# Windowed attention and routed experts on one core: the exponentials of a tile one step later in ScalarE's queue, and all products with the values ahead of the turned exponentials on TensorE

## The chip, the cores and the metric

The kernel runs on 1 core of one Trainium2 chip. The time is the device time of one execution in microseconds (us). Five engines have a queue each and work through it in order: TensorE (PE; its weight loads are listed as PEld), VectorE (DVE), ScalarE (ACT), GpSimd (POOL) and SyncE (SP, which here only issues DMAs).

## The reference

```python
# attention, q k v: (8, 8, 576, 64), window 64
scores = scale * q @ k^T ; kept where 0 <= row - col < 64
attn = softmax(scores) ; out = attn @ v
# routed experts on x = out as (4608, 512)
logits = xn @ en.T / tau ; expert_idx = argmax(logits)
out[mask] = gate_w[mask, None] * (max(x[mask] @ w1[e], 0) @ w2[e])
```

## The kernel before, in words

The 4608 tokens are 36 tiles of 128. The program is laid out by hand: `stages(s)` (L538) emits, for s = 0 to 34, one step of a software pipeline over the tiles, and every engine runs its instructions in the order of emission. After the loop an epilogue, also written out by hand, ends the last tiles between the first products of the experts. Then come the experts, group by group, each product as three of split operands (L916, L976).

A tile T goes through these stations, each with the step s in which it is emitted:

- s = T: `scores` (L213, PE, into the one PSUM tile `score`), `own_scores` (L220, ACT, copies the half of the scores that belongs to the tile's own keys), `all_scores` (L223, DVE, puts the other half in by a mask), `maxima` (L227, DVE), `less_max` (L231, POOL, subtracts the maximum in place), `exponentials` (L234, ACT, in place). The exponentials are the last but one thing that ScalarE gets in the step (in eight even steps, 14 to 28, a copy of a weight half for the experts, L629, follows; VectorE then subtracts it, L630).
- s = T + 1: `attn_transposes` (L243, PE, turns the exponentials into the PSUM tile `back`), `attn_copy` (L253, ACT), `attn_prev` (L256, DVE) and `attn_own` (L259, POOL, in place on what `attn_copy` wrote), which make the two masked operands.
- s = T + 2: `values_other` (L279, PE, needs `attn_prev`), `values_mine` (L293, PE, needs `attn_own`), then `x_out` (L317, L318, L321, DVE, divides by the sums).
- s = T + 3: `x_transposes` (L336, PE, into `xback`), `xT_evac` (L342, ACT), `squares` (L329, ACT). Later: logits, the choice of an expert (`choose`, L400 to L404, DVE), ranks (L421 to L425, PE; L456 to L471, DVE) and `place`, an indirect DMA of the row to its expert's place (L480, POOL). `choose` and the ranks come once in four steps for tiles 0 to 27.

In a step s TensorE's order is `scores(s)`, at times `logits_four`, `values_other(s-2)`, `attn_transposes(s-1)`, `x_transposes(s-3)`, small products of the routing, `values_mine(s-2)`. ScalarE's is `own_scores(s)`, `attn_copy(s-1)`, `xT_evac(s-3)`, `squares(s-3)`, the issue of a load of k, `exponentials(s)`, at times the weight copy. VectorE's is `all_scores(s)`, `maxima(s)`, `attn_prev(s-1)`, `x_out(s-2)`, the routing's work, at times L630. GpSimd's is `less_max(s)`, `attn_own(s-1)`, `place`, and once in four steps small routing work. SyncE issues the loads of q, v and the weights.

Of the kernel before, what the change touches and what calls it, by code (L numbers as in the profile page):

```python
# [27 lines left out]
NT = N // P  # L28
# [55 lines left out]
def attention_moe(ctx, tc, q, k, v, emb, tau, w1, w2, kc, kt, out):  # L84
# [83 lines left out]
    def load_q(T, engine=nc.sync):  # L168
        if T < NT:
            engine.dma_start(qT[:, T % RQ], q[T].rearrange("p (u c) -> p u c", u=4))  # L170
# [5 lines left out]
    def load_v(T):  # L176
        if T < NT:
            nc.sync.dma_start(vb[:, T % RV], v[T])

    def vblock(g):  # L180
        return vb[:, g // 2 % RV, g % 2]
# [4 lines left out]
    def scores(T):  # L186

        for z in range(2):
            if (2 * T + z) % NB == 0:
                for hp in range(2):  # L190
                    o = score[64 * z:64 * z + 64, hp].rearrange("p (u c) -> p u c", u=4)[:, :, :WIN]
                    nc.tensor.matmul(o, lhsT=ones[64 * hp:64 * hp + 64, :64],
                                     rhs=low[64 * hp:64 * hp + 64].rearrange("p (u c) -> p u c", u=4),
                                     start=True, stop=True)
        at = T % RK * KT
        for u in range(4):
            for hp, z in sides:
                pr, o = slice(64 * hp, 64 * hp + 64), score[64 * z:64 * z + 64, hp, u * P:(u + 1) * P]
                qz = qT[pr, T % RQ, u, z * WIN:(z + 1) * WIN]
                own = kT[pr, at + u * P + z * WIN:at + u * P + (z + 1) * WIN]  # L200
                if (2 * T + z) % NB == 0:
                    parts = [(o[:, WIN:], own)]
                elif z:
                    parts = [(o, kT[pr, at + u * P:at + (u + 1) * P])]
                else:
                    was = (T - 1) % RK * KT + u * P + WIN
                    if at:
                        hop = KT - WIN
                        parts = [(o, kT[pr, was:was + 2 * hop].rearrange("p (a c) -> p a c", a=2)[:, :, :WIN])]
                    else:  # L210
                        parts = [(o[:, :WIN], kT[pr, was:was + WIN]), (o[:, WIN:], own)]
                for to, keys in parts:
                    nc.tensor.matmul(to, lhsT=qz, rhs=keys, start=True, stop=True)  # L213
# [4 lines left out]
    def own_scores(T):  # L218
        sm[T] = ap.tile([P, 4, 2, WIN], F32, name="sm", bufs=3)
        nc.scalar.copy(sm[T], sv[:, :, :, 1])  # L220
# [12 lines left out]
    def exponentials(T):  # L233
        nc.scalar.activation(sm[T], sm[T], AF.Exp, scale=0.125)  # L234
# [3 lines left out]
    def attn_transposes(T):  # L238

        pT[T] = back.rearrange("p (u c) -> p u c", u=4)  # L240
        t = sm.pop(T).rearrange("p u h c -> p u (h c)")
        for u in range(4):
            nc.tensor.transpose(pT[T][:, u], t[:, u], ident)  # L243
# [7 lines left out]
    def attn_copy(T):  # L251
        aM[T] = ap.tile([P, 2, 4, P], F32, name="aM", bufs=2)
        nc.scalar.copy(aM[T][:, 0], pT[T])  # L253
# [15 lines left out]
    def values_other(T):  # L269

        px[T] = banks_of(T)
        other = aM[T][:, 1]
        g = 2 * T
        for u in range(4):
            for hp, z in sides:
                if z == 0 and g % NB == 0:
                    continue
                pr, pz = slice(64 * hp, 64 * hp + 64), slice(64 * z, 64 * z + 64)
                nc.tensor.matmul(px[T][hp][pz, u * (D + 1):(u + 1) * (D + 1)], lhsT=other[pr, u, pz],  # L279
                                 rhs=vblock(g - 1 + 2 * z)[pr, u], start=u == 0, stop=(g + z) % NB == 0 and u == 3)  # L280

    def values_mine(T):

        mine = aM.pop(T)[:, 0]
        g = 2 * T
        first = [(g + z) % NB == 0 for z in range(2)]
        halves_ = slice(0, 64), slice(64, P)
        for u in range(4):
            rows = halves_[:1] if first[1] else halves_ if first[0] or u > 1 else [slice(0, P)]
            for hp in range(2):  # L290
                pr = slice(64 * hp, 64 * hp + 64)
                for pz in rows:
                    nc.tensor.matmul(px[T][hp][pz, u * (D + 1):(u + 1) * (D + 1)], lhsT=mine[pr, u, pz],  # L293
                                     rhs=vblock(g)[pr, u], start=u == 0 and first[0] and pz.start == 0, stop=u == 3)
# [59 lines left out]
    def logits_four(G):  # L354

        a, b = GROUPS[G]
        for c in range(4):
            for T in range(a, b):
                j = 32 * (T - a)
                nc.tensor.matmul(plT[j:j + 32], lhsT=embT[:, c], rhs=xT[T][:, c], start=(c == 0), stop=(c == 3))  # L360

    def four_copy(G):
        turned_back[G] = ap.tile([P, P], F32, name="lT", bufs=1)
        nc.scalar.copy(turned_back[G], plT)

    def four_back(G):
        nc.tensor.transpose(plq.rearrange("p g e -> p (g e)"), turned_back.pop(G), ident)
# [165 lines left out]
    def warm(n, to=back):  # L533

        for _ in range(n):
            nc.tensor.matmul(to[:, :P], lhsT=ones, rhs=ones, start=True, stop=True)

    def stages(s):  # L538

        def there(d):  # L540
            return 0 <= s - d < NT

        def ending(d):
            return [G for G, (a, b) in enumerate(GROUPS) if b + d == s]

        def turned():
            if there(1):
                attn_transposes(s - 1)
                attn_copy(s - 1)

        scores(s)
        if s < 3:
            warm(12, side[1])
        own_scores(s)
        if s == 33:
            x_hi(0)
        four = [G for G in ending(3) if len(range(*GROUPS[G])) == 4]
        for G in four:
            logits_four(G)
            four_copy(G)  # L560
        load_q(s + RQ)
        if there(2):
            values_other(s - 2)
        load_v(s + RV - 3)
        for f in wsteps.get(s, ()):
            f()
        if s > 3:
            turned()
        if there(3):
            x_transposes(s - 3)  # L570
        for G in four:
            four_back(G)
        if s - 4 in (28, 29):
            logits(s - 4, side[(s + 1) % 2][:, :E])
        due = [G for G, (a, b) in enumerate(GROUPS) if s == (b + 5 if b - a == 4 else b + 4)]
        for G in due:
            if len(range(*GROUPS[G])) == 4:
                ranks(G)
        if there(2):
            values_mine(s - 2)  # L580
        all_scores(s)
        maxima(s)
        if s < 3:
            warm(12, side[1])
        if there(3):
            xT_evac(s - 3)
        for G in four:
            four_out(G)
        if s - 4 in (28, 29):
            nc.scalar.copy(x_rows(s - 4, s - 3)[:, 0, C_LOG:C_LOG + E], side[(s + 1) % 2][:, :E])  # L590
        less_max(s)
        if there(3):
            squares(s - 3)
        load_k(s + RK - 1, nc.scalar)
        if s > 3:
            attn_prev(s - 1)
            attn_own(s - 1)
        for G in due:
            if len(range(*GROUPS[G])) == 4:
                rank_base(G)  # L600
        if there(2):
            x_out(s - 2)
        if s in (32, 33):
            x_turned(s - 32)
        if 0 < s <= 3:
            turned()
            attn_prev(s - 1)
            attn_own(s - 1)
        for G in due:
            if len(range(*GROUPS[G])) == 2:  # L610
                ranks(G)
            ranks_out(G)
        for G, (a, b) in enumerate(GROUPS):
            for T in range(a, b):
                if s == (T + 9 if b - a == 4 else b + 4):
                    place(T)
        if s == 33:
            x_lo(0)
        for G in ending(3):
            choose(G)  # L620
            tokens(G)
            count(G)
        exponentials(s)
        if s == 33:
            x_hi(1)
            x_lo(1)
        if s in wsplit:
            c, at = wsplit[s]
            nc.scalar.copy(w1h[c][:, at], w1raw[c][:, at])  # L629
            nc.vector.tensor_tensor(out=w1l[c][:, at], in0=w1raw[c][:, at], in1=w1h[c][:, at].bitcast(F32), op=ALU.subtract)  # L630
        if 1 <= s < 7:
            blanks(s - 1)
# [175 lines left out]
    def x_hi(a):  # L808
        xh, xl, t = x_half(a)
        nc.scalar.copy(xh, t)  # L810
# [509 lines left out]
```

## Time and profile before

| | us |
|---|---|
| median of 3 runs (lowest, highest) | 628.2 (624.93, 630.13) |
| the profiled execution | 622.73 |
| its span in the profile | 621.0 |
| PE busy in the span | 593.6 (96%) |
| DVE, ACT, POOL busy | 429.5, 354.7, 232.4 |

The profile is of one execution. A busy time counts when an engine has an instruction under way. The loop over the tiles takes about the first 160 us, and the experts the rest. The granted TensorE clock is shown as a share of full speed.

### The profile page before, as it was taken

The page shows a single profiled execution, that of the slowest core. Times are in us where ns is not written, and L with a number is a line of the kernel's source. Part 1 is how long each engine was busy: PE and PEld are TensorE (multiplying, and loading weights), DVE is VectorE, ACT ScalarE, POOL GpSimd, SP SyncE. Part 2 cuts the span into 40 slices and gives each one's busy share as a digit, 9 for nine tenths or more (in the row PEclk, how much of TensorE's full clock was granted, in tenths as well). Part 3 has the DMA queues.
Part 4 walks back from the last instruction along what each step waited for, and adds up shares of the span by engine and source line. Part 5 has one row for each costly group of instructions (what it writes and reads, how often), then busy time and mean ns, then how long its engine had stood idle before and what let it go on. Part 6 is the DMA issues. An engine that isn't in the chain of part 4 may idle for free. (4 is left out here: it accounts for less than half of the span.)

```text
span 621.0 us, 17807 instructions
## 1 busy us (share of the span) xinstructions
PE 593.6 (96%) x6836; PEld 528.8 (85%) x6836; DVE 429.5 (69%) x883; ACT 354.7 (57%) x567; POOL 232.4 (37%) x224
## 2 busy tenths in 40 slices
PE   8899988889899999999999999999999999999995
PEld 7687777778799898989988999899889998998884
DVE  2778888888888658686566775756765677657623
ACT  3566766666542447466466664645676466636533
POOL 2567878787833133213203331142122331222011
PEclk9999999999999999999999999999999999999999
DMA  8887888885535588886786897839778877775351
GB/s 270 276 228 238 298 264 267 244 253 152 202 114 204 134 275 279 241 269 243 245 283 208 265 295 257 271 132 327 249 242 246 277 267 222 245 262 196 114 168 38
DMA packets 85789, 143.75 MB, mean 231 GB/s; under 512 B 15797, under 2 KB 36021, under 8 KB 85696
## 3 DMA queue, kind: packets, MB, share of 16 engines
q1 hardware_dynamic: 74560, 112.87, 58.0%
q0 software_dynamic: 6000, 19.18, 8.1%
q10 hardware_dynamic: 5136, 10.49, 5.6%
q8 instruction: 55, 0.90, 0.6%
q14 instruction: 38, 0.31, 0.2%
HBM read 123.23 MB, written 20.05 MB: 231 GB/s over the span
## 5 line engine op out<-in xcount | busy, mean ns | idle before, releaser
L916 PE MATMUL ph<-xh,w1h 128*128 128x256 f32 x576 | 162.0, 281 | 1.3 <-DVE rk L456 1.3
L916 PE MATMUL ph<-xh,w1l 128*128 128x256 f32 x576 | 161.9, 281 | 1.0 <-DVE w1l L159 1.0
L916 PE MATMUL ph<-xl,w1h 128*128 128x256 f32 x576 | 161.4, 280 | 0.3 <-POOL xl L814 0.3
L988 POOL DMA_INDIRECT out<-o,rest x39 | 49.3, 1265 | 219.9 <-ACT o L985 206.3
L976 PE MATMUL po<-w2h,hh 128*128 128x512 f32 x312 | 122.2, 392 | 0.0
L976 PE MATMUL po<-w2h,hl 128*128 128x512 f32 x312 | 121.8, 390 | 0.0
L976 PE MATMUL po<-w2l,hh 128*128 128x512 f32 x312 | 121.6, 390 | 0.0
L930 DVE SCALAR_TENSOR_TENSOR hl<-ph,hh 128x512 fp32r<-128x512 f32 x78 | 53.4, 689 | 92.9 <-ACT hh L926 92.7
L159 DVE TENSOR_TENSOR w2l<-w2raw,w2h 128x1024 fp32r<-128x1024 f32 x80 | 94.7, 1220 | 24.3 <-ACT w2h L156 24.0
L916 PEld LDWEIGHTS ph<-xh,w1h 128*128 128x128 f32 x576 | 108.1, 188 | 2.1 <-issue 1.4
L916 PEld LDWEIGHTS ph<-xh,w1l 128*128 128x128 f32 x576 | 108.3, 188 | 1.6 <-DVE w1l L159 1.4
L916 PEld LDWEIGHTS ph<-xl,w1h 128*128 128x128 f32 x576 | 108.3, 188 | 1.4 <-POOL xl L814 0.5
L156 ACT CAST w2h<-w2raw 128x1024 fp32r<-128x1024 f32 x80 | 81.5, 1049 | 39.7 <-PE po L976 32.0
L159 DVE TENSOR_TENSOR w1l<-w1raw,w1h 128x1024 fp32r<-128x1024 f32 x76 | 89.2, 1236 | 11.0 <-ACT w1h L156 10.3
L814 POOL TENSOR_TENSOR xl<-xt,xh 128x512 fp32r<-128x512 f32 x37 | 47.8, 1293 | 100.4 <-ACT xh L810 100.4
L926 ACT ACTIVATE hh<-ph 128x512 fp32r<-128x512 f32 x78 | 46.1, 595 | 57.1 <-PE ph L916 43.4
L156 ACT CAST w1h<-w1raw 128x1024 fp32r<-128x1024 f32 x76 | 73.9, 1047 | 0.0
L976 PEld LDWEIGHTS po<-w2h,hl 128*128 128x128 f32 x312 | 58.6, 188 | 12.6
L976 PEld LDWEIGHTS po<-w2l,hh 128*128 128x128 f32 x312 | 58.6, 188 | 11.5
L976 PEld LDWEIGHTS po<-w2h,hh 128*128 128x128 f32 x312 | 58.6, 188 | 11.5
L810 ACT CAST xh<-xt 128x512 fp32r<-128x512 f32 x39 | 24.1, 620 | 54.6 <-DVE xt L799 53.9
L231 POOL TENSOR_TENSOR sm<-sm,st 128x512 f32<-128x512 f32 x36 | 37.5, 1041 | 36.1 <-DVE st L227 31.6
(208 smaller groups left out, 836.1 us busy)
## 6 DMA issues: line engine op xcount, KB each, us to landing
w2raw<-in_w SPq DMA_DIRECT2D x76, 512.0 KB
w1raw<-in_w SPq DMA_DIRECT2D x72, 512.0 KB
xb<-xs SPq DMA_DIRECT2D x156, 64.0 KB
v<-in_v SPq DMA_DIRECT2D x36, 260.0 KB
qT<-in_q SPq DMA_DIRECT2D x36, 256.0 KB
kT<-in_k ACTq DMA_DIRECT2D x32, 256.0 KB
w1raw<-in_w SPq DMA_DIRECT2D x8, 256.0 KB
w2raw<-in_w SPq DMA_DIRECT2D x8, 256.0 KB
```

The source lines that it names most:

```text
L156: nc.scalar.copy(hi[c], raw[c])
L159: eng.tensor_tensor(out=lo[c], in0=raw[c], in1=hi[c].bitcast(F32), op=ALU.subtract)
L231: nc.gpsimd.tensor_tensor(out=t, in0=t, in1=st.pop(T).unsqueeze(2).to_broadcast([P, 8, WIN]), op=ALU.subtract)
L810: nc.scalar.copy(xh, t)
L814: eng.tensor_tensor(out=xl, in0=t, in1=xh.bitcast(F32), op=ALU.subtract)
L916: nc.tensor.matmul(o, lhsT=ww[c][:, f * P:(f + 1) * P], rhs=xx[:, c, :n], start=(c == 0 and i == 0), stop=(c == 3 and i == 2))
L926: nc.scalar.activation(hh, ph[g, part], AF.Relu)
L930: nc.vector.scalar_tensor_tensor(out=hl, in0=ph.pop((g, part)), scalar=0.0, in1=hh.bitcast(F32), op0=ALU.max, op1=ALU.subtract)
L976: nc.tensor.matmul(po[a], lhsT=xx[:, f, at], rhs=ww[f // 2][:, f % 2], start=(f == 0 and i == 0), stop=(f == 7 and i == 2))
L988: d = nc.gpsimd.indirect_dma_start(out=out, out_offset=bass.IndirectOffsetOnAxis(ap=tok, axis=0), in_=o, in_offset=None, bounds_check=N - ...
```

## The change

`exponentials(s)` is no longer emitted at the end of step s, but in step s + 1 right behind `own_scores(s + 1)`, for tiles 3 to 33 (tiles 0 to 2 and 34 stay where they were). `values_mine(s - 2)`, which stood behind the transposes and the routing's small products, is emitted right behind `values_other(s - 2)`, ahead of `attn_transposes(s - 1)`. So ScalarE's order in a step becomes `own_scores(s)`, `exponentials(s-1)`, `attn_copy(s-1)`, `xT_evac(s-3)`, `squares(s-3)`, and TensorE's becomes `scores(s)`, `values_other(s-2)`, `values_mine(s-2)`, `attn_transposes(s-1)`, `x_transposes(s-3)`. VectorE's, GpSimd's and SyncE's orders stay.

```diff
         own_scores(s)
+        if s > 3:
+            exponentials(s - 1)
         if s == 33:
             x_hi(0)
...
         for f in wsteps.get(s, ()):
             f()
+        if there(2):
+            values_mine(s - 2)
         if s > 3:
             turned()
...
             if len(range(*GROUPS[G])) == 4:
                 ranks(G)
-        if there(2):
-            values_mine(s - 2)
         all_scores(s)
         maxima(s)
...
             count(G)
-        exponentials(s)
+        if s < 3 or s == NT - 2:
+            exponentials(s)
```

## Rows read from the trace of the kernel before

**Rows 1.** Busy time of each engine in three stretches: in the loop over the tiles, and in two behind it. Columns: stretch and its length, busy time (instructions) of each engine, granted TensorE clock, share of the DMA engines, GB/s.

```profile
69.60:137.80 68.20, 60.01 (x1619) 50.55 (x1614) 57.91 (x136) 46.97 (x106) 53.93 (x54) 1.00 0.85 258
...
165.00:185.00 20.00, 19.89 (x353) 18.15 (x352) 15.74 (x52) 9.37 (x18) 9.88 (x16) 1.00 0.39 125
185.00:240.00 55.00, 53.96 (x377) 49.02 (x376) 40.38 (x131) 24.89 (x38) 16.05 (x15) 1.00 0.67 213
```

**Rows 2.** Who waited for whom in the loop (27.5 to 160 us): total us, times, longest.

```profile
ACT sm L234 <- POOL sm L231: 31.7, 29, 1.9
...
PE back L243 <- ACT sm L234: 7.2, 19, 0.5
```

**Rows 3.** The subtraction of the maximum on GpSimd in steps 4, 14, 29 and 33, from the timeline (start us, duration us); it marks the pace.

```profile
27.50 1.04 POOL L231 TENSOR_TENSOR sm<-sm,st 128x512 f32<-128x512 f32 x1 [1.36 <-DVE st L227]
...
69.58 1.04 POOL L231 TENSOR_TENSOR sm<-sm,st 128x512 f32<-128x512 f32 x1
...
137.76 1.04 POOL L231 TENSOR_TENSOR sm<-sm,st 128x512 f32<-128x512 f32 x1 [0.64 <-DVE st L227]
...
155.07 1.03 POOL L231 TENSOR_TENSOR sm<-sm,st 128x512 f32<-128x512 f32 x1 [0.95 <-DVE st L227]
```

**Rows 4.** The timeline of one step (scores of tile 24 at 110.09 us), all engines, instructions in order of start; a run of alike instructions is one row.

```profile
109.21 1.06 PE L293 MATMUL odd<-v,aM 64*128 64x65 f32 x24
...
110.09 1.05 PE L213 MATMUL score<-kT,qT 64*64 64x128 f32 x32
...
110.92 0.69 DVE L321 TENSOR_TENSOR xmore<-odd,sums 128x512 f32<-128x512 f32 x1
110.96 0.65 PE L279 MATMUL even<-v,aM 64*64 64x65 f32 x32
111.07 1.27 POOL L259 TENSOR_TENSOR aM<-aM,cs 128x512 f32<-128x512 f32 x1
111.13 0.63 ACT L234 ACTIVATE sm<-sm 128x512 f32<-128x512 f32 x1 [0.63 <-POOL sm L231]
...
111.53 0.18 DVE L400 TENSOR_REDUCE m<-xr 128x4 f32<-128x32 f32 x1
...
111.67 0.57 ACT L220 COPY sm<-score 128x512 f32<-128x512 f32 x1
111.74 0.65 DVE L401 TENSOR_TENSOR c<-xr,m 128x32 f32<-128x32 f32 x1
...
111.81 0.66 PE L243 MATMUL back<-cs,sm 128*128 128x128 f32 x4 [0.21 <-ACT sm L234]
...
112.51 0.59 ACT L253 COPY aM<-back 128x512 f32<-128x512 f32 x1 [0.27 <-PE back L243]
...
112.84 0.54 PEld L293 LDWEIGHTS even<-v,aM 64*64 64x64 f32 x16 [0.17 <-issue]
...
112.98 0.72 DVE L223 COPY_PREDICATED sm<-cs,score 128x512 f32<-128x512 uint32 x1
112.99 0.59 ACT L342 COPY xfour<-xback 128x512 f32<-128x512 f32 x1
...
113.47 0.64 ACT L329 ACTIVATE sq<-xmore 128x512 bf16<-128x512 f32 x1
...
113.81 0.69 DVE L227 TENSOR_REDUCE st<-sm 128x8 f32<-128x512 f32 x1
...
114.41 0.68 DVE L256 TENSOR_TENSOR aM<-back,cs 128x512 f32<-128x512 f32 x1
114.57 1.04 POOL L231 TENSOR_TENSOR sm<-sm,st 128x512 f32<-128x512 f32 x1 [0.66 <-DVE st L227]
115.01 0.16 DVE L317 TENSOR_SCALAR sums<-even 128x8 f32<-128x8 f32 x1
...
115.44 0.69 DVE L321 TENSOR_TENSOR xmore<-even,sums 128x512 f32<-128x512 f32 x1
115.57 1.27 POOL L259 TENSOR_TENSOR aM<-aM,cs 128x512 f32<-128x512 f32 x1
```

**Rows 5.** VectorE's part of the ranks, which comes once in four steps, and the mask that follows it, from the timeline.

```profile
101.45 0.18 DVE L456 TENSOR_TENSOR rk<-even,cs 128x32 f32<-128x32 f32 x1
...
102.59 0.76 DVE L465 TENSOR_TENSOR rk<-rk,oh 128x32 f32<-128x32 f32 x1
...
103.68 0.72 DVE L223 COPY_PREDICATED sm<-cs,score 128x512 f32<-128x512 uint32 x1
```

**Rows 6.** The weight copy and its subtraction in the loop, by line (27.5 to 160 us): form, count, busy us and mean ns, idle time before.

```profile
L630 DVE TENSOR_TENSOR w1l<-w1raw,w1h 128x512 fp32r<-128x512 f32 x8 | 5.5, 692 | 6.8 <-ACT w1h L629 6.2 <-DMA kT<-in_k 0.7
L629 ACT CAST w1h<-w1raw 128x512 fp32r<-128x512 f32 x8 | 4.8, 604 | 0.0
```

**Rows 7.** Step 3, in which `attn_copy` and `attn_prev` of tile 2 were late, from the timeline.

```profile
24.21 0.59 ACT L253 COPY aM<-back 128x512 f32<-128x512 f32 x1 [2.51 <-DMA qT<-in_q]
...
24.83 0.69 DVE L256 TENSOR_TENSOR aM<-back,cs 128x512 f32<-128x512 f32 x1 [1.52 <-ACT aM L253]
```

**Rows 8.** The product of L465 with GpSimd idle (the first row; GpSimd's `attn_own` had ended at 157.34) and with GpSimd's queue full (the second), and the GpSimd instruction that ended just before the second did, from the timeline.

```profile
157.43 0.15 DVE L465 TENSOR_TENSOR rk<-rk,oh 128x32 f32<-128x32 f32 x1
...
162.09 2.95 DVE L465 TENSOR_TENSOR rk<-rk,oh 128x16 f32<-128x16 f32 x1
...
163.72 1.27 POOL L259 TENSOR_TENSOR aM<-aM,cs 128x512 f32<-128x512 f32 x1
```

## The prediction

> **What bounds the kernel now.** I read the stretches first. Behind the loop TensorE has no room: it is busy 19.89 of 20.00 us and 53.96 of 55.00 us at the full clock [rows 1]. So what the loop loses or gains is passed on to the end one for one, and only the loop has to be worked out. In the loop no engine is full: of 68.20 us TensorE is busy 60.01, VectorE 57.91, GpSimd 53.93, ScalarE 46.97 [rows 1]. A stretch like that is paced by a loop of waits through several engines. The waits say where: ScalarE stood 31.7 us in 29 steps with the exponentials at the head of its queue, waiting for GpSimd's subtraction, and TensorE 7.2 us in 19 steps for the exponentials [rows 2].
>
> The loop is read from one step [rows 4], from start to start: exponentials to the next own-scores copy 111.67 - 111.13 = 0.54 (the copy stands behind them in the queue, and its scores had been ready since 110.09 + 1.05 = 111.14), copy to mask 0.57 + 0.05, mask to maxima 113.81 - 112.98 = 0.83, maxima to subtraction 114.57 - 113.81 = 0.76, subtraction to exponentials 1.04 + 0.04. Sum 3.83 us per step. VectorE's work for the routing and the weight copy come on top. The pace shows it: steps 4 to 14 and 29 to 33, without weight copies, take (69.58 - 27.50 + 155.07 - 137.76) / 14 = 4.24 us, or 16.97 for four steps; steps 14 to 29 take (137.76 - 69.58) / 15 = 4.545, or 18.18 for four [rows 3].
>
> **The change, part by part.**
>
> *Removed.* The own-scores copy no longer stands behind the exponentials, so the loop of 3.83 us is cut, and so is the weight copy's 0.60 us [rows 6], which stood in it between the two. The exponentials' own work (0.63) is the same. DMA issues keep their order: the load of k was and is issued behind the squares, the loads of q and v on SyncE's own queue.
>
> *Added.* `values_mine` now stands ahead of the transposes and needs `attn_own`. GpSimd runs `attn_own` of the tile before right behind the subtraction: 111.07 + 1.27 = 112.34, while `values_other` is through at 110.96 + 0.65 = 111.61 [rows 4]. So at the old pace TensorE waits 0.73 us there; before, it waited 0.21 us (0.38 in the mean, 7.2 / 19, [rows 2]) for the exponentials. Behind the waiting products stand the transposes, the x transposes and the next scores; the exponentials themselves are ready in time and cost nothing, hidden under this wait and the 0.88 us of `values_mine`.
>
> *The new loop.* It spans two steps: mask, maxima, subtraction, `attn_own`, `values_mine`, transposes, `attn_copy`, `attn_prev`, `x_out`, next mask but one. Start to start [rows 4]: 0.83 + 0.76 + 1.00 (114.57 to 115.57) + 1.27 + 0.05 (a handover) + 0.88 (`values_mine` to the next block, 109.21 to 110.09) + 0.70 (111.81 to 112.51) + 0.59 + 0.05 + 0.60 (114.41 to 115.01) + 0.43 (115.01 to 115.44) + 0.61 (110.92 to 111.53) = 7.77 us, or 15.54 for four steps.
>
> VectorE's routing work lies in it once in four steps each. Ranks: 0.18 and from L465 to the mask 103.68 - 102.59 = 1.09 [rows 5]; choice: 112.98 - 111.53 = 1.45 [rows 4]; together 2.72. Part of that is not work: L465 takes 0.15 when GpSimd is idle, 0.76 beside `attn_own` and 2.95 until GpSimd's queue has a gap [rows 5, 8], so 0.61 of its time and about 0.65 - 0.15 = 0.50 of L401's [rows 4] is blocking by GpSimd. Without it: 2.72 - 1.11 = 1.61. Four quiet steps then take 17.15 to 18.26. Both shares are likely to stay in part, since `attn_prev` comes later against `attn_own`; I take the middle, 17.7: 0.73 more than 16.97. There are 14 such steps, 3.5 fours: +2.6 us.
>
> The two waits in which `attn_prev` stands for `attn_copy` are the weak point of this sum: the timeline shows it plainly in step 3, where DVE idled 1.52 us and started at 24.83, right after the copy's end at 24.80 [rows 7]; elsewhere the copy was done long before. If it holds in every step, the loop is 7.77; if not, 0.59 + 0.05 fall out, 1.28 per four steps, and the quiet steps end at 16.4, a gain of 2.0 us. By the Trainium skill (PSUM — Partial Sum Buffer, "PSUM bank collisions raise a hardware error") two engines may not touch one bank and quadrant at once, two reads included, so a copy on ScalarE and a product on VectorE out of `back` have to be kept apart in every tile: by that rule the sum is the first. The row agrees in the one step where it can be seen, and I keep the first by the row.
>
> *Steps with weight copies.* Here the loop can go through ScalarE: `values_mine` 0.88, transposes to x copy 112.99 - 111.81 = 1.18, to the squares 113.47 - 112.99 = 0.48, squares 0.64 [rows 4], weight copy 0.60 + 0.05, subtraction on VectorE 0.69 [rows 6], then 0.83 + 0.76 + 1.00 + 1.27 + 0.05 as above: 8.43 for two steps, 16.9 for four. L630 now comes while `attn_own` runs, has two inputs in SBUF like L465, and would be blocked like it by some 0.6: 18.1. The loop through the ranks (17.15 to 18.26) runs beside it and the slower sets the pace, so the bounds are 17.15 and 18.26; I take 18.1, because the rows show blocking whenever such an add met `attn_own`. That is 0.1 less than 18.18 for 3.75 fours: -0.4 us.
>
> **Sum:** +2.6 - 0.4 = +2.2 us. On the profiled execution: 622.73 + 2.2 = 624.9 (its span 621.0 + 2.2 = 623.2); it lies 5.5 us under the median of the runs shown. On that median: 628.2 + 2.2 = 630.4 us.
>
> **The rivals.**
>
> 1. *TensorE's new wait counts in full* (slower). The 0.73 us take the place of 0.38, and every step is 0.35 longer: 29 steps x 0.35 = +10.2, 638.4 us. For it: TensorE is the busiest engine of the loop. Against it: the copy of the scores started 0.53 us after its scores were done [rows 4], so a later TensorE has that slack first. It decides from the point at which the scores end later than VectorE comes free for their mask.
>
> 2. *The lock the other way round* (slower). L630 starts first and GpSimd's adds stand for it, up to 0.69 in 8 steps [rows 6] on the subtraction's path: +5.5 on top of +2.2, 635.9 us. For it: VectorE's adds and GpSimd's do exclude each other [rows 5, 8]; against it: the rows show only VectorE as the one that waits. The Trainium skill (SBUF — State Buffer, "Who interferes with whom") has the port pair go to whoever issues first, whole, so by it this is possible; no run here shows it.
>
> 3. *The loop is cut and nothing takes its place* (faster). Then TensorE's own queue paces: start to start 0.87 + 0.85 (110.96 to 111.81 at most) + 1.03 (111.81 to 112.84) + 0.88 = 3.6, and about 0.3 per step for the small products, 3.9 for 29 steps against (155.07 - 27.50) / 29 = 4.40: -14.5, 613.7 us. Against it: `attn_own` ends 0.73 us behind `values_other` already.
>
> 4. *A smaller gain*: `attn_prev` doesn't wait for the copy and L630 isn't blocked: -2.0 and (16.9 - 18.18) x 3.75 = -4.8 (were the loop through the ranks also without the copy): -6.8, 621.4 us at the most; half of it is more likely, 625.
>
> **How the numbers follow.** About 1% (6.3 us) is what a measurement of this kernel can tell from no change. Chances: the forecast 0.58; rival 1 0.15; rival 2 0.07; rival 3 0.07; rival 4 0.13, of which 0.04 past 1%. So faster 0.07 + 0.04 = 0.11, slower 0.15 + 0.07 = 0.22, same 0.67. The likeliest gives 630.4. Its own bounds: low +0.18 x 3.5 - 1.03 x 3.75 = -3.2; high +1.29 x 3.5 + 0.08 x 3.75 = +4.8, and 0.17 us for the issue of `values_mine` [rows 4] in each loop of two steps, 14.5 x 0.17 = +2.5: 625.0 to 635.5. Widened towards rivals 1 and 4 and for the spread of the runs: 623.5 to 637.5.
>
> **What would show it.** ScalarE's wait at L234 for L231 should all but vanish (from 31.7 us), TensorE's for L234 too; a new wait of L293 for L259 of 0.3 to 1.0 us per step should stand in their place; L256 should wait for L253 in most steps; the quiet steps should take about 4.4 us, those with weight copies about 4.5, and everything behind 162 us should keep its length. It is wrong if the pace of the loop changes by more than 0.2 us per step either way, if L293 doesn't wait, or if the experts' part changes by more than 2 us.

## The result, and the profile after

The kernel after takes 631.8 us in the median of 20 runs, the kernel before 628.66 us beside it: ratio 1.0061 with a 95% interval of 1.0045 to 1.0078, that is 3.8 us longer (2.8 to 4.9). The ratio goes by the means, 632.2 and 628.4 us, without one of the 20 runs of after, which took 1465.84 us; so it says a little more than the medians, which lie 3.1 us apart. The forecast was 630.4 us, +2.2. A second series gave 632.35 us and 1.0058 (1.0040 to 1.0077).

The profiled executions don't show this number: their spans are 621.0 us before and 628.3 us after. Why they lie further apart is answered by a second profile of each kernel below. The loop is to be read first, and there the two waits of [rows 2] are gone and others stand in their place. First the waits of the kernel after in the same stretch, 27.5 to 160 us (total us, times, longest):

```profile
ACT aM L253 <- PE back L243: 39.1, 27, 2.3
DVE aM L256 <- ACT aM L253: 12.8, 16, 2.1
...
PE odd L293 <- POOL aM L259: 6.9, 9, 1.1
...
PE even L293 <- POOL aM L259: 5.0, 9, 1.0
```

and three groups of its instructions there, by line (form, count, busy us and mean ns, idle time before, ended by whom); lines from 555 on stand two or three further down than before, so L632 and L633 answer to L629 and L630:

```profile
L234 ACT ACTIVATE sm<-sm 128x512 f32<-128x512 f32 x29 | 18.7, 644 | 0.4 <-POOL sm L231 0.2
L633 DVE TENSOR_TENSOR w1l<-w1raw,w1h 128x512 fp32r<-128x512 f32 x8 | 9.6, 1203 | 0.0
...
L465 DVE TENSOR_TENSOR rk<-rk,oh 128x32 f32<-128x32 f32 x6 | 2.2, 363 | 0.0
```

ScalarE's wait for the subtraction fell from 31.7 us to 0.2. Its idle time now lies ahead of the next copy (39.1 us at L253, for the transposes, where before it was 5.4): the same engine waits as long as before (31.7 + 5.4 us), one instruction later. TensorE, which had waited 7.2 us for the exponentials, waits 6.9 + 5.0 = 11.9 us in 18 steps for `attn_own`. VectorE waits 12.8 us in 16 steps for `attn_copy`; in the kernel before that was 0.2 us in all.

The pace, by the subtraction in steps 4, 14, 29 and 33 as in [rows 3] (start us, duration us):

```profile
26.70 1.04 POOL L231 TENSOR_TENSOR sm<-sm,st 128x512 f32<-128x512 f32 x1 [1.33 <-DVE st L227]
...
71.58 1.05 POOL L231 TENSOR_TENSOR sm<-sm,st 128x512 f32<-128x512 f32 x1
...
140.00 1.03 POOL L231 TENSOR_TENSOR sm<-sm,st 128x512 f32<-128x512 f32 x1 [0.70 <-DVE st L227]
...
157.54 1.03 POOL L231 TENSOR_TENSOR sm<-sm,st 128x512 f32<-128x512 f32 x1 [0.42 <-PE back L243]
```

Steps 4 to 33 take 157.54 - 26.70 = 130.84 us, before 127.57: +3.3. The 14 quiet steps take (44.88 + 17.54) / 14 = 4.46 us each, 17.83 for four (before 16.97); the 15 with weight copies 68.42 / 15 = 4.56, 18.25 for four (before 18.18). The start of the pipeline gave 0.8 us back: step 4 comes at 26.70, not 27.50.

The busy times in the three stretches of [rows 1]:

```profile
69.60:137.80 68.20, 59.96 (x1590) 50.74 (x1588) 59.90 (x136) 45.78 (x107) 52.72 (x53) 1.00 0.80 255
165.00:185.00 20.00, 19.19 (x317) 17.56 (x314) 14.56 (x37) 7.46 (x15) 12.39 (x16) 0.97 0.26 99
185.00:240.00 55.00, 53.37 (x432) 48.07 (x430) 38.30 (x142) 22.55 (x36) 14.74 (x16) 1.00 0.62 186
```

TensorE's 59.96 of 68.20 us is that of before, GpSimd's 52.72 is 1.2 less; only VectorE is up, from 57.91 to 59.90 us, above all by the subtraction of the weight copy (L633, 1.20 us where L630 took 0.69), which now runs beside GpSimd's products. No engine became the bound: the loop of waits did. It can be walked in the timeline of two steps (start us, duration us, in brackets the idle time before and who ended it):

```profile
42.87 0.73 DVE L223 COPY_PREDICATED sm<-cs,score 128x512 f32<-128x512 uint32 x1
...
43.71 0.69 DVE L227 TENSOR_REDUCE st<-sm 128x8 f32<-128x512 f32 x1
...
44.54 1.04 POOL L231 TENSOR_TENSOR sm<-sm,st 128x512 f32<-128x512 f32 x1 [1.26 <-ACT xfour L342]
...
45.54 1.27 POOL L259 TENSOR_TENSOR aM<-aM,cs 128x512 f32<-128x512 f32 x1
...
46.87 1.05 PE L293 MATMUL odd<-v,aM 64*128 64x65 f32 x24 [1.12 <-POOL aM L259]
...
47.85 0.66 PE L243 MATMUL back<-cs,sm 128*128 128x128 f32 x4
48.55 0.58 ACT L253 COPY aM<-back 128x512 f32<-128x512 f32 x1 [2.30 <-PE back L243]
49.23 0.69 DVE L256 TENSOR_TENSOR aM<-back,cs 128x512 f32<-128x512 f32 x1 [1.78 <-ACT aM L253]
...
50.37 0.69 DVE L321 TENSOR_TENSOR xr<-odd,sums 128x512 f32<-128x512 f32 x1
...
50.98 0.18 DVE L465 TENSOR_TENSOR rk<-rk,oh 128x32 f32<-128x32 f32 x1
...
51.49 0.73 DVE L223 COPY_PREDICATED sm<-cs,score 128x512 f32<-128x512 uint32 x1
```

From start to start: 0.84 + 0.83 + 1.00 + 1.33 + 0.98 + 0.70 + 0.68 + 1.14 + 1.12 = 8.62 us for two steps, with one set of ranks in it (L456, 0.18 us at 49.84, of which 0.11 lies in this sum, and 50.98 to 51.49). Without the ranks it is 8.00. These are the stations that the prediction named, in its order; its own terms, with the unblocked ranks, came to 7.77 + 0.66 = 8.43.

Behind the loop one thing differs that the prediction did not name. In step 34 ScalarE's queue, TensorE's wait and the granted clock of three stretches of 3.4 us look like this in the kernel after:

```profile
160.88 0.62 ACT L813 CAST xh<-xt 128x512 fp32r<-128x512 f32 x1 [1.47 <-DVE xt L802]
...
161.40 0.58 ACT L220 COPY sm<-score 128x512 f32<-128x512 f32 x1
...
161.88 0.63 ACT L234 ACTIVATE sm<-sm 128x512 f32<-128x512 f32 x1
...
162.56 0.91 PE L243 MATMUL back<-cs,sm 128*128 128x128 f32 x4 [1.50 <-ACT sm L234]
```

```profile
159.40:162.80 3.40, 1.91 (x66) 1.63 (x59) 3.19 (x14) 1.65 (x4) 1.09 (x2) 1.00 0.94 318
162.80:166.20 3.40, 3.40 (x62) 3.31 (x60) 2.67 (x8) 1.79 (x4) 3.37 (x7) 0.50 0.26 99
166.20:169.60 3.40, 3.40 (x58) 3.13 (x51) 2.51 (x3) 2.05 (x3) 3.16 (x3) 0.99 0.02 5
```

The exponentials of tile 33 were moved not only past `own_scores(34)` but past a cast of the expert's input (L813), which waited 1.47 us for VectorE. TensorE waited 1.50 us for them, was busy 1.91 of 3.40 us, and then ran for 3.4 us at half the full clock (1.2 instead of 2.4 GHz). The profile of before has no such fall until 618.8 us.

Two stretches behind the loop are longer than before. The subtraction of step 34 in the kernel before (first row), and in the kernel after (third row), with the `attn_prev` that comes ahead of it there:

```profile
162.72 1.04 POOL L231 TENSOR_TENSOR sm<-sm,st 128x512 f32<-128x512 f32 x1
...
158.16 0.69 DVE L256 TENSOR_TENSOR aM<-back,cs 128x512 f32<-128x512 f32 x1 [0.78 <-ACT aM L253]
...
166.06 1.03 POOL L231 TENSOR_TENSOR sm<-sm,st 128x512 f32<-128x512 f32 x1
```

and the products `values_other` of tile 33, the first behind the loop, in the kernel before (first row) and after:

```profile
167.39 0.70 PE L279 MATMUL odd<-v,aM 64*64 64x65 f32 x32
...
171.07 0.61 PE L279 MATMUL odd<-v,aM 64*64 64x65 f32 x18
172.07 0.37 PE L279 MATMUL odd<-v,aM 64*64 64x65 f32 x6 [0.39 <-issue]
172.85 0.38 PE L279 MATMUL odd<-v,aM 64*64 64x65 f32 x8 [0.42 <-issue]
```

From the subtraction of step 33 to that of step 34 it is 7.65 us before and 8.52 after. From the first of these products to the start of `values_mine` (168.02 before, 173.16 after) it is 0.63 and 2.09 us; "issue" says that the profile names nothing that TensorE waited for.

### The profile page after: what moved, and what is told of

Same layout as the page of the kernel before. It is cut to its first block, busy times and chain, and to the rows that moved or that the text cites. A ratio compares the mean times of both kernels' runs of the same rounds, so it can differ in the third digit from the quotient of the medians.

```text
span 628.3 us, 17866 instructions
## 1 busy us (share of the span) xinstructions
PE 599.2 (95%) x6836; PEld 533.7 (85%) x6836; DVE 428.9 (68%) x883; ACT 353.0 (56%) x567; POOL 233.0 (37%) x224
## 4 chain that ended last, share of the span: by engine, by line
PE 57%; issue 4%; DMA 3%; DVE 2%; POOL 1%; ACT 1%; POOLq 0%; ACTq 0%; another core or an unknown queue 0%; DVEq 0%
PE po L979 28%; PE ph L919 27%; PE ph L956 2%; DMA w1raw<-in_w 1%; DMA out<-o,rest 1%; POOL out L991 0%; DVE w1l L159 0%; DVE xt L802 0%; DMA xb<-xs 0%; POOL xl L817 0%; PE ph L965 0%; ACT xh L813 0%; POOLq L1319 0%; POOL gsm L836 0%; ACT w1h L156 0%
## 5 line engine op out<-in xcount | busy, mean ns | idle before, releaser
L979 PEld LDWEIGHTS po<-w2h,hl 128*128 128x128 f32 x312 | 58.6, 188 | 12.5
L813 ACT CAST xh<-xt 128x512 fp32r<-128x512 f32 x39 | 24.2, 619 | 56.3 <-DVE xt L802 54.5
L231 POOL TENSOR_TENSOR sm<-sm,st 128x512 f32<-128x512 f32 x36 | 37.5, 1041 | 38.0 <-DVE st L227 23.9
```

The costliest lines, as they stand in the source:

```text
L231: nc.gpsimd.tensor_tensor(out=t, in0=t, in1=st.pop(T).unsqueeze(2).to_broadcast([P, 8, WIN]), op=ALU.subtract)
L979: nc.tensor.matmul(po[a], lhsT=xx[:, f, at], rhs=ww[f // 2][:, f % 2], start=(f == 0 and i == 0), stop=(f == 7 and i == 2))
```

## The experiments

The ratios are to the kernel before, with 95% intervals. The "loop" is steps 4 to 33 as above: 127.6 us before, 130.8 after.

**The end of the loop.** Against the kernel after, tile 33 gets its exponentials at the old place:

```diff
-        if s > 3:
+        if 3 < s < NT - 2:
             exponentials(s - 1)
...
-        if s < 3 or s == NT - 2:
+        if s < 3 or s >= NT - 3:
             exponentials(s)
```

> The change as it is, but the exponentials of tile 33 stay at the end of step 33, ahead of x_hi(1) in ScalarE's queue. Theory (the loop over the tiles costs about 2.5 us, and the rest is that tile 33's exponentials now stand behind x_hi(1), which waits for VectorE's transposes): TensorE's 1.5 us wait at L243 in step 34 goes, the clock stays at its upper level there, and the time falls by 1.5 to 3 us against the changed kernel, to 1.001 to 1.004 of the kernel before. Rival (the end of the loop differs in that one profiled execution by chance): 1.006 as for the changed kernel.

Measured: 632.68 us, 1.0080 (1.0052 to 1.0109); loop 132.2. Nothing was won. The 1.50 us wait at L243 is gone, but TensorE then waits 1.3 us for the ranks (L456) a little later, and there are falls of the clock at 65.9 and 168.3 us. Step 34 takes 8.52 us as in the kernel after. The theory that the move past the cast costs the end of the loop some microseconds fell.

**One part of the change alone.** First the later exponentials without the earlier `values_mine` (against before):

```diff
         own_scores(s)
+        if s > 3:
+            exponentials(s - 1)
...
-        exponentials(s)
+        if s < 3 or s == NT - 2:
+            exponentials(s)
```

> Only the exponentials move; values_mine stays last in TensorE's step. Theory (two loops of waits, no single engine full): the exponentials' own loop is cut, but the transposes come right behind own scores and exponentials and the products with the values behind them, so the loop over the tiles is 1 to 2.5 us longer and the end of the loop 1 to 2 us: 1.003 to 1.007. Rival 1 of the prediction (TensorE's new wait for attn_own counts in full): without that wait the change can only gain, 0.98 to 1.000.

Measured: 628.55 us, 1.0025 (1.0005 to 1.0046); loop 128.8. Its waits in the loop:

```profile
ACT sm L220 <- PE score L213: 14.8, 23, 1.2
PE back L243 <- ACT sm L234: 14.6, 21, 0.8
```

The transposes now stand directly on the later exponentials: 14.6 us of TensorE's waiting where before there were 7.2. So the one half gains nothing: a wait of ScalarE became one of TensorE. The time lies just under the theory's 1.003 to 1.007 and above the rival's.

Then the earlier `values_mine` without the later exponentials (against before):

```diff
+        if there(2):
+            values_mine(s - 2)
         if s > 3:
             turned()
...
-        if there(2):
-            values_mine(s - 2)
         all_scores(s)
```

> Only values_mine moves ahead of the transposes; the exponentials stay at the end of the step. Theory: TensorE waits for attn_own where it waited for the exponentials, own scores still stand behind the exponentials; steps without weight copies lengthen by about 0.15 us, the others hardly: +2 to +2.5 us, 1.003 to 1.004, and no loss at the end of the loop. Rival 1 (the wait counts in full, 0.35 us in 29 steps): 1.016.

Measured: 634.19 us, 1.0102 (1.0076 to 1.0128); loop 132.6, one fall of the clock in it. Its waits:

```profile
PE odd L293 <- POOL aM L259: 6.5, 8, 1.1
PE even L293 <- POOL aM L259: 6.0, 9, 1.0
...
ACT sm L234 <- POOL sm L231: 2.7, 6, 0.7
```

This half alone is worse than the whole, and worse than the theory gave it; with it alone TensorE waits for `attn_own` 12.5 us, as in the whole (11.9), and ScalarE's 31.7 us shrink to 2.7 without any move of the exponentials, because ScalarE already waits 37.0 us for the transposes ahead of `attn_copy`. So the larger cost comes with `values_mine`. That the later exponentials take a part of it back is likely but not shown: the intervals of this half (1.0076 to 1.0128) and of the whole (1.0045 to 1.0078) touch.

**GpSimd's product in two halves.** If TensorE waits for `attn_own`, half of it done early might shorten the wait. Against after:

```diff
-        nc.gpsimd.tensor_tensor(out=aM[T][:, 0], in0=aM[T][:, 0], in1=halves[:, 0].unsqueeze(1).to_broadcast([P, 4, P]), op=ALU.mult)
+        for u in (0, 2):
+            o = aM[T][:, 0, u:u + 2]
+            nc.gpsimd.tensor_tensor(out=o, in0=o, in1=halves[:, 0].unsqueeze(1).to_broadcast([P, 2, P]), op=ALU.mult)
```

> The changed kernel, with attn_own as two instructions of half the size, so that the first half of values_mine can start after the first. Theory (the wait of values_mine for attn_own is in the two-step loop that paces): each half shortens the loop by some 0.5 us per two steps if a half takes 0.64 us on GpSimd, -6 us against the changed kernel, 0.996 to 0.998 of the kernel before; with 0.70 us per half -3.5 us, 1.000; with 0.75 or more nothing is won. Rival (the loop of attn_prev's wait for the copy paces, without attn_own): no change against the changed kernel, 1.006.

Measured: 632.62 us, 1.0074 (1.0049 to 1.0099). The halves by line (they stand at L261), and TensorE's waits for them:

```profile
L261 POOL TENSOR_TENSOR aM<-aM,cs 128x256 f32<-128x256 f32 x58 | 42.4, 752 | 1.0 <-ACT aM L253 0.8
```

```profile
PE odd L295 <- POOL aM L261: 5.2, 13, 0.7
...
PE even L295 <- POOL aM L261: 1.5, 6, 0.5
```

TensorE's waiting falls from 11.9 to 6.7 us, but the two halves take 2 x 0.75 = 1.50 us where the whole took 1.27, and the time is that of after. The loop had two falls of the clock (102.5 and 140.0 us), so its 132.8 can't be set beside 130.8. The theory had said that nothing is won from 0.75 us per half on, so this run doesn't decide between it and its rival. A shorter wait at one place is no gain while the loop is not shorter.

**The clock at the end of the loop.** 24 extra small products of TensorE fill its wait in step 34. Against after:

```diff
+        if s == NT - 2:
+            warm(24)
         if s > 3:
             turned()
```

> The changed kernel with 24 small products of constants (128 columns each) on TensorE in step 34, ahead of the transposes of tile 33, where TensorE stood idle for 1.5 us before its clock fell to half for 3.4 us. Theory (part of the loss is TensorE's clock: the new waits leave it idle long enough at a stretch that it is granted 1.2 GHz for a while): no fall of the clock behind step 34, and 1 to 2 us less than the changed kernel, 1.003 to 1.005 of the kernel before. Rival (all of the loss is the pace of the loop): 1.006 to 1.008, as the changed kernel, or more by the added work.

Measured: 630.99 us, 1.0058 (1.0036 to 1.0081); loop 131.1. Two of the stretches as above; the clock of this execution fell at 182.8 us only, before the end of the experts:

```profile
159.40:162.80 3.40, 3.35 (x99) 2.97 (x89) 3.16 (x15) 1.88 (x5) 1.10 (x2) 1.00 1.04 392
162.80:166.20 3.40, 2.86 (x63) 2.55 (x63) 2.93 (x8) 1.70 (x4) 3.37 (x6) 1.00 0.42 158
```

With TensorE busy 3.35 of 3.40 us the clock stays at full where it had fallen, and the time is the same: the fall at 162.8 is not what makes the change slower.

**Without `attn_own`.** If the loop goes through it, the change must gain once it is gone. `attn_own(s - 1)` is struck in both of its places, from after (first) and from before (second):

```diff
-            attn_own(s - 1)
```

> The changed kernel without attn_own: values_mine takes the unmasked copy, so the attention is not the reference's and tokens go to other experts; only the pace of the loop is read, steps 4 to 33 (127.6 us in the kernel before, 130.8 in the changed one). Theory (the two-step loop through attn_own replaced the loop through the exponentials): without attn_own both are gone, and the stretch takes about 116 us. Rival (the loop of attn_prev's wait for the copy paces by itself): 128 us or more.

> The kernel before without attn_own, in the same way; steps 4 to 33 are read. Theory (in the kernel before, attn_own lies in no loop, but it blocks VectorE's adds with two inputs in SBUF, some 1.1 us in four steps, and holds back GpSimd): about 121 us, so that the change alone gains some 5 us once attn_own is out of the way. Rival 1 of the prediction (TensorE's waits alone count): 127.6 us as before.

Measured (only the loop is read): after 123.95 us, before 127.87. Without `attn_own` the change gains 3.9 us, with it it loses 3.3. Some 1.4 of the 3.9 are one stall of the kernel before: at 67.06 us TensorE stood 2.26 us in the midst of a run of L279, held by nothing that the profile names, and the step behind it took 6.01 us where its like take 4.56 to 4.58. The 2.5 us that are left still turn the sign: the product that `values_mine` now meets decides it. But both loops are 7 to 8 us longer than the theory said; 123.95 lies between theory and rival. In the kernel before four quiet steps fell to 16.5 us, but those with weight copies rose to 18.7, 0.4 of it by the stall. What sets the pace of these two kernels is open.

**Before once more.** One more profile of the unchanged kernel before:

> The kernel before once more, for a second profile. Theory: steps 4 to 33 take 127 to 128 us again, and the clock stays at its upper level until the end of the experts. Rival (falls of the clock come by chance in either kernel): one or more falls between 27 and 200 us.

Measured: 631.12 us, span 629.3, loop 156.67 - 27.73 = 128.9. Two stretches of it:

```profile
162.00:165.60 3.60, 2.01 (x33) 1.67 (x26) 3.50 (x6) 0.19 (x1) 3.60 (x7) 1.00 0.45 171
165.60:172.40 6.80, 6.80 (x80) 6.22 (x82) 4.57 (x11) 2.48 (x5) 5.30 (x7) 0.50 0.30 119
```

The same program has a span of 621.0 us once and 629.3 us another time. As the rival said, its clock was at half in 25.6 to 29.0, 165.6 to 172.4 and 182.7 to 186.1 us; every step of the loop but the one at the first fall (5.45 instead of 4.01 us) had the pace of the first profile to 0.15 us. So the 7.3 us between the two spans shown at first are no measure of the change: the profile of before was an execution without falls, and the kernel before has them as well.

**Both products on VectorE.** The kernel has a function (`attn_halves`, L245) that makes both masked operands in one VectorE product and needs neither `attn_copy` nor GpSimd. It takes the place of the three, in after (first) and in before (second):

```diff
-                attn_copy(s - 1)
...
-            attn_prev(s - 1)
-            attn_own(s - 1)
+            attn_halves(s - 1)
```

> The changed kernel with attn_halves (one VectorE instruction that makes both masked operands, 1.22 us) in place of attn_copy, attn_prev and attn_own: nothing of tile T stands behind GpSimd's subtraction any more, at 0.54 us more on VectorE per step. Theory (the loop through attn_copy and attn_own is what makes the change lose; cutting the loop through the exponentials is worth something once that one is gone): steps 4 to 33 take about 123.5 us against 131 of the changed kernel, the run 0.992 to 0.995 of the kernel before. Rival 1 of the prediction (any wait of TensorE counts in full): values_mine waits less, about 0.99 as well. Rival (the loss comes from the exponentials' later place itself, or from VectorE's load): 1.006 or more.

> The kernel before with attn_halves in the same place. Theory (in the kernel before, the loop through the exponentials paces, and GpSimd's and VectorE's work beside it counts only through VectorE's queue: 0.54 us more of VectorE's work against some 1.1 us of blocking in four steps): steps 4 to 33 take 127 to 128 us, 0.998 to 1.002. Rival (taking attn_own out of GpSimd's queue is a gain by itself, whatever the order): as the changed kernel with attn_halves, 0.992 to 0.995.

Measured: on after 630.33 us, 1.0030 (1.0013 to 1.0047), loop 126.6; on before 633.34 us, 1.0067 (1.0044 to 1.0091), loop 131.0. The change gains 4.5 us in the loop here, where about 4 were expected. But both loops are some 3 us longer than expected, and both times lie above the theory's 0.992 to 0.995 and 0.998 to 1.002: on after the loop is 1.0 us shorter than in the kernel before, and the run still 1.9 us longer. Where behind the loop that is lost was not followed up. VectorE is busy 63.08 and 61.09 of 68.20 us in the loops:

```profile
69.60:137.80 68.20, 63.18 (x1635) 54.20 (x1631) 63.08 (x139) 39.94 (x94) 33.06 (x39) 1.00 0.84 262
```

```profile
69.60:137.80 68.20, 60.88 (x1590) 51.26 (x1590) 61.09 (x133) 39.24 (x89) 32.69 (x39) 1.00 0.81 251
```

**After once more.** The counterpart to the second profile of before:

> The changed kernel once more. Theory (the loss is the pace of the loop, +3.0 us of 128; falls of the clock come by chance in both kernels): steps 4 to 33 take 130.5 to 132 us, 1.004 to 1.007 of the kernel before. Rival (the clock's falls make the loss): the stretch takes 128 to 129 us where the clock stays up.

Measured: 632.35 us, 1.0058 (1.0040 to 1.0077), span 631.3; loop 130.85 us against 130.84 in the first profile. As the theory said, the pace of the loop repeats, to a hundredth; the falls of the clock (162.9 and 197.0 us here) don't.

**The product shared out.** By all this, `attn_own` should be shorter and stay where it is. VectorE masks half of it straight out of `back` behind `attn_prev`, and ScalarE copies and GpSimd masks the other half. Against after:

```diff
-        nc.scalar.copy(aM[T][:, 0], pT[T])
+        nc.scalar.copy(aM[T][:, 0, 2:], pT[T][:, 2:])
...
-        nc.vector.tensor_tensor(out=aM[T][:, 1], in0=pT.pop(T), in1=halves[:, 1].unsqueeze(1).to_broadcast([P, 4, P]), op=ALU.mult)
+        nc.vector.tensor_tensor(out=aM[T][:, 1], in0=pT[T], in1=halves[:, 1].unsqueeze(1).to_broadcast([P, 4, P]), op=ALU.mult)
+        nc.vector.tensor_tensor(out=aM[T][:, 0, :2], in0=pT.pop(T)[:, :2], in1=halves[:, 0].unsqueeze(1).to_broadcast([P, 2, P]), op=ALU.mult)
...
-        nc.gpsimd.tensor_tensor(out=aM[T][:, 0], in0=aM[T][:, 0], in1=halves[:, 0].unsqueeze(1).to_broadcast([P, 4, P]), op=ALU.mult)
+        nc.gpsimd.tensor_tensor(out=aM[T][:, 0, 2:], in0=aM[T][:, 0, 2:], in1=halves[:, 0].unsqueeze(1).to_broadcast([P, 2, P]), op=ALU.mult)
```

> The changed kernel with the own mask shared out: VectorE makes the first two of its four parts out of PSUM (about 0.4 us more per step), ScalarE copies and GpSimd masks the other two (0.73 us in place of 1.27). Theory (the wait of values_mine for attn_own paces the changed kernel): the first half of values_mine no longer waits for GpSimd, the two-step loop is 0.9 to 1.2 us shorter less 0.4 us of VectorE's per step; steps 4 to 33 take 124 to 127 us against 130.8, the run 0.993 to 0.999 of the kernel before. Rival (VectorE's load decides): 128 us or more, 1.003 to 1.006.

Measured: 626.01 us against 629.39 of before, 0.9951 (0.9932 to 0.9970), loop 126.5, both as the theory said. It beats both kernels. The ends of its loop, its busy times, and the shared product by line:

```profile
26.75 1.04 POOL L231 TENSOR_TENSOR sm<-sm,st 128x512 f32<-128x512 f32 x1 [1.75 <-DVE st L227]
...
153.24 1.04 POOL L231 TENSOR_TENSOR sm<-sm,st 128x512 f32<-128x512 f32 x1 [1.35 <-DVE st L227]
```

```profile
69.60:137.80 68.20, 62.71 (x1662) 53.36 (x1657) 61.29 (x157) 45.60 (x109) 46.48 (x55) 1.00 0.84 264
```

```profile
L260 POOL TENSOR_TENSOR aM<-aM,cs 128x256 f32<-128x256 f32 x30 | 22.0, 732 | 0.6 <-ACT aM L253 0.6
...
L257 DVE TENSOR_TENSOR aM<-back,cs 128x256 f32<-128x256 f32 x31 | 12.8, 414 | 0.0
...
L253 ACT COPY aM<-back 128x256 f32<-128x256 f32 x30 | 11.2, 373 | 38.7 <-PE back L243 34.3 <-DVE st L227 1.6 <-PE even L368 1.6
```

The loop is 126.5 us, 4.3 less than after: 0.54 us less of GpSimd (1.27 to 0.73) and 0.21 less of ScalarE (0.58 to 0.37), against 0.41 more of VectorE. It shortens two links of the loop at once, so it doesn't say what `attn_own` alone is worth. TensorE's wait for GpSimd's product, 11.9 us in after, is 0.2. Not all of the 3.4 us under before is the loop (1.1 by the first profile): the mean granted clock of its timed runs was 0.994, of the runs of before beside them 0.990.

## Why the prediction was right

**Removed: right.** In the loop ScalarE's wait at L234 and TensorE's for it vanished, and with them the copy's place behind the exponentials. Without `attn_own`, or with it on VectorE, the change gains 3.9 (2.5 without the stall) and 4.5 us in the loop: the cut of the old loop is real.

**Added: right in place, less even than said.** `values_mine` waits for `attn_own` up to 1.1 us, in 18 of 29 steps, 11.9 / 18 = 0.66 in the mean. The forecast had 0.73 and 0.3 to 1.0. Rival 1, by which these waits count in full, gives 638.4 and is out for the whole change. The run with the earlier values alone (1.0102) lies nearer to it: 634.2 us, between the sum and the rival. Of its some 6 us 132.6 - 127.6 = 5.0 lie in the loop, a part of them by the fall of the clock; why that part alone costs more than the whole is not settled.

**The new loop: right, its weak point too.** The sum stood or fell with `attn_prev` waiting for `attn_copy`. It does, in 16 of 29 steps: 12.8 us, and 1.78 of VectorE's idle time in the two steps shown. No run takes this wait away alone, with `attn_prev` ahead of the copy. The Trainium skill (PSUM — Partial Sum Buffer, "PSUM bank collisions raise a hardware error") has the two reads of one bank kept apart, and the trace agrees: 49.23 is the end of the copy at 48.55 + 0.58 = 49.13 and a handover.

**The size: a little small, and near by some luck.** Quiet steps took 17.83 us for four where the sum had 17.7, those with copies 18.25 where it had 18.1: +3.0 + 0.3 = +3.3 instead of +2.6 - 0.4 = +2.2. The mis-sized term is the base loop: 8.00 against 7.77 for two steps, by the one walk above. The links that grew most are `values_mine` to the transposes (0.98 for 0.88) and maxima to subtraction (0.83 for 0.76). The routing adds went the other way, near the lower bound: L465 took 0.36 us in the mean (0.67 before) and L401 some 0.2 (0.65), so of the 1.11 us of blocking about 0.25 stayed, where the middle had kept half. The two errors nearly cancel: 2 x 8.00 + 1.61 + 0.25 = 17.86, and 17.83 was measured. One more thing holds the loop up in both kernels, and the sum left it out: GpSimd's queue has `place` ahead of the subtraction. In the step behind the walk the maxima were through at 53.01, `place` at 53.71, and the subtraction started at 53.74. Such steps are 6 of 29 before (0.4 to 0.75 us) and 8 after (0.4 to 1.0); what they cost was not tested.

**The weight copy: right in size, not in its path.** L633 was blocked as forecast, 1.20 us for 0.69, and the gain that rival 4 hoped for there is not to be had. But the loop that the prediction built for these steps, from the squares over the weight copy on ScalarE to the subtraction, is not what paced them: VectorE was never idle ahead of L633 (0.0 us, the row above), where it had waited 6.2 us for the copy ahead of L630 [rows 6]. L633 stands behind `x_out` in VectorE's queue; which waits pace these steps is open. GpSimd's subtraction was not the one that waited (L231 keeps its 1.04 us, L259 its 1.27), so rival 2 did not come. The Trainium skill (SBUF — State Buffer, "Who interferes with whom") would allow it; no run here shows it.

**Behind the loop: missed.** The prediction counted 29 steps and kept everything behind 162 us. Of the 3.8 us (2.8 to 4.9), 157.54 - 155.07 = 2.5 are there when the loop ends, and two places behind it grew, each by the same amount in both profiles of after. In step 34 it is 8.52 - 7.65 = 0.87 us: `attn_prev` of tile 32 waits 0.78 us for the copy, which is the wait of the loop once more, in a step that the sum didn't count. In the products of tile 33 it is 2.09 - 0.63 = 1.46 us, by gaps for which the profile names no cause; why they stand there and not in the kernel before is open. Together that is 4.8 us. The move past the cast in step 34, which the prediction overlooked as well, is not the cause: step 34 is as long without it. Nor is the clock on average: its mean was 0.992 in the 64 executions of before that were timed beside the experiments and 0.9935 in 19 of after. By the slope given at the end, an estimate, the higher clock of after hides some 0.6 us, so that at one clock the change would cost about 4.4.

**The anchor.** The sum was made against an execution of 622.73 us and then put on the median. That was the safe way: the execution was one without falls of the clock, some 6 us under the median of the later runs.

## What to carry to other kernels

When a move frees one loop of waits, write down the loop that the moved instruction closes at its new place, start to start through every engine; here the freed loop (3.83 us a step) gave way to one of 8.6 us for two steps, and the sign hung on one GpSimd product in it. Then shorten that product rather than move more: halving it and giving the other half to an engine that was already there turned +3.8 us into -3.4. And set spans of single profiles beside each other only stretch by stretch; two executions of one program lay 8.3 us apart here.

## What the runs showed of the hardware that was not expected

- The granted TensorE clock falls to half for 3.4 us, or 6.8, at places that change from one execution to the next: none until 618.8 us in the first profile of before, three before 200 us in the second; at 162.8 and 162.9 us in the two of after. Ahead of those at 162.8 and 165.6 TensorE had been busy 1.91 of 3.40 and 2.01 of 3.60 us. Over 64 executions of before, a mean clock lower by 0.01 went with a time longer by 3.2 us.
- A GpSimd product of 128x512 takes 1.27 us and one of 128x256 0.73 to 0.75: two halves cost 0.2 us more than the whole.
- A two-input VectorE add of 128x512 takes 1.20 us beside GpSimd's products, and 0.69 where it didn't meet them [rows 6]; GpSimd's own durations don't change (1.03 to 1.08 us for the subtraction, 1.26 to 1.30 for the whole `attn_own`, in all runs).
- TensorE can stand still in the midst of a run of like products, held by nothing that the profile names: mostly some 0.4 us a time, in every trace here, and 2.26 us at 67.06 us in the kernel before without `attn_own`. In the two profiles of after the gaps at 172 us come at the same place, to 0.04 us.
